# Where the stores of the sums of w_out are issued in the last pair of token tiles

## The chip, the cores and the metric

The kernel runs as one program on one core of a Trainium2 chip. The metric is the device time of one execution in microseconds (us), as a median over runs. Five engines each work through an instruction queue of their own in order: PE multiplies matrices, DVE (vector) and ACT (scalar) do elementwise work, POOL (GpSimd) a little of it, and SP only issues DMA transfers. An instruction waits in its queue until what it depends on has signalled, and everything behind it on that engine waits with it.

## The reference

An attention without a square matrix, and then a feed-forward layer:

```
q = softmax(q) over the 64 features of a head;  k = softmax(k) over the 576 positions
kv[b,h] = k^T v            (64 x 64 for each of 8 batches x 8 heads)
x = q kv, heads side by side:  4608 tokens x 512
h = x w_in                 (512 x 2048)
g = softplus(h)
out = g w_out              (2048 x 512)
```

All is float32. PE takes operands split in two parts, a high one (rounded to fp32r) and a low one (the remainder); three matmuls of parts (high by high, high by low, low by high) stand for one product.

## The kernel before

The 4608 tokens are nine tiles of 512 (numbers 0 to 8). Tiles 0 to 2 go one by one; tiles 3 to 8 go in pairs (3,4), (5,6), (7,8). In a pair the products with w_in are made in a scheme of seven products in place of eight for two by two blocks, on sums of blocks; the sums of w_in are made once and kept in DRAM. **In the last pair alone, (7,8), the products with w_out are made so too.** This needs, for each pair p of chunks of the hidden size (p = 0 to 7), four sums of blocks of w_out, "the sums of w_out", made by `turn_steps` (lines 1185 to 1211):

- `T0.p`, `whole_parts` (L1194): high plus low part of the loaded w_out, into a work tile called `two`, of which there is one
- `T1.p`, `combine` (L1199): four subtractions in that tile
- `T2.p`, `split` (L1204 on ACT, L1205 on DVE): a new tile `turned[p]` of 1 MB, in slot `x0` for even p and `x1` for odd p; ACT writes its high part, then DVE its low part
- `T3.p`, `store` (L1209 on SP): `turned[p]` to DRAM, for p = 0 to 5 alone, as `turn`

For p = 5, 6, 7 POOL does T0 and T1, and DVE otherwise. Tile 7's products read `turned[p]` one pass later (L1286). Tile 8's products come at the end of the kernel; for p = 0 to 5 they read the sums again from DRAM, loaded by step `R{p}` (`load_sources`, L1294 and L1295), which first waits until the two slots that it fills are free.

The work is written out as a sequence. The last pair runs in eight passes p = 0 to 7 of four steps k = 0 to 3, and after them come the products that are left. In each step PE's products with w_in (L1137) are issued, then the names in the plan's string ahead of its bar, then the products with w_out of the pass before (L1286), then the names behind the bar. The plan of the last pair is the third list in `PAIRS`; its first 32 strings are the steps of the eight passes. Each engine gets its instructions in the order in which the sequence calls them. In step 1 of a pass SP also issues the load of w_in's sums called `low` (L1073), in step 3 the load called `top` (L1073) ahead of the string and the load `down` of w_out (L1080) behind the products. A load waits for its slot to be free.

A slot is given to a new tile once all accesses to the old tile are done, also those that come later in the sequence than the new tile's first write: so T2.2's write to `x0` waits for the landing of store T3.0, though T3.0 stands behind it in the plan. The other names in the strings: S, J and L take w_in's products out of PSUM (L1398 ACT, L1401 DVE, L1404 and L1408 ACT), `a` and `e` make the operands of tiles 7 and 8 (L1239 ACT, L1240 and L1252 DVE), `v` adds up results (L1306 DVE).

Of the kernel before, what the change touches and what calls it, by code (L numbers as in the profile page):

```python
# [186 lines left out]
        "S3.1 J3.1|T1.1 v2.0",  # L187
        "a3.0 T2.1 L4.1|a0.1 a1.1 J2.1",
        "|S1.2 J1.2 a2.1 v3.0",
        "L3.1 L1.2 S2.2 T3.1 T0.2|",  # L190
        "S3.2 T1.2 J3.2|",
        "a3.1 L4.2 J2.2 v2.1 T2.2 L2.0|a0.2 T3.0",
        "|v3.1 T0.3 S1.3 J1.3 L2.1 a1.2 T1.3 a2.2 L1.3",
        "|S2.3 T2.3",
        "S3.3|J3.3",
        "v2.2 a3.2 L4.3|J2.3 a0.3",
        "T0.4 a1.3 S1.4 T3.3 T1.4 L2.3 J1.4 v3.2 a2.3 T3.2 e0.0 L3.3|",
        "S2.4 L2.2|",
        "|S3.4 J3.4 a3.3 v2.3",
        "|L1.4 J2.4 a0.4 L4.4",  # L200
        "T2.4 S1.5|J1.5",
        "v3.3 a1.4|S2.5",
        "L3.4 L2.4 a2.4 T3.4 S3.5 T0.5 J3.5|L3.2 T1.5",
        "e1.0 a3.4 T2.5 L1.5 v2.4 J2.5|v3.4 L4.5 a0.5",
        "S1.6 J1.6|",
        "L2.5 a1.5 S2.6|a2.5",
# [2 lines left out]
        "L1.6 T0.7 a0.6 L2.6 R0 v3.5 a1.6 S1.7 J1.7 L3.6 e0.6|T1.7 a2.6",  # L209
        "T2.7|S2.7 a3.6",  # L210
        "L1.7|S3.7 J3.7 e1.6 v2.6",
        "L4.7 T3.5 e2.6|J2.7",
        "L3.7 a0.7 a1.7 a2.7 R2 v3.6 a3.7|",
        "|",
        "|",
        "|",
        "e3.6|",
        "|",
        "L2.7|e0.7 T3.7 T3.6",
        "|",  # L220
        "|",
        "|e1.7",
# [72 lines left out]
def tile_attn_ffn(  # L295
# [362 lines left out]
    def eight(name, shape, dtype=F32):  # L658
        return (xp if name[0] == "x" else wp).tile(shape, dtype, name=name)
# [175 lines left out]
    with tc.manual_schedule():  # L835
# [127 lines left out]
        def dram(name, k, shape):  # L963
            drams[name, k] = dp.tile([P, *shape], F32, name=f"{name}{k}")
            return drams[name, k]
# [220 lines left out]
        def turn_steps(p, w):  # L1186

            work = []

            def whole_parts():  # L1190
                work.append(qp.tile([P, 2, TOK], F32, name="two").rearrange("p c (k n) -> p (c k) n", k=2))
                d = downs[w].bitcast(F32)
                y = work[0].rearrange("p (c k) n -> p c (k n)", c=2)
                (nc.gpsimd if p in TURN_POOL else nc.vector).tensor_tensor(out=y, in0=d[:, :, 0], in1=d[:, :, 1], op=ALU.add)  # L1194

            def combine():
                y = [work[0][:, i] for i in range(4)]
                for out, in0, in1 in ((0, 1, 0), (1, 3, 1), (3, 3, 0), (2, 3, 2)):
                    (nc.gpsimd if p in TURN_POOL else nc.vector).tensor_tensor(out=y[out], in0=y[in0], in1=y[in1], op=ALU.subtract)  # L1199

            def split():
                turned[p] = eight(f"x{p % 2}", [P, 2, 4, 256], F32R)
                hi, lo = (turned[p][:, i] for i in range(2))
                nc.scalar.copy(hi, work[0])  # L1204
                nc.vector.tensor_tensor(out=lo, in0=work[0], in1=hi.bitcast(F32), op=ALU.subtract)  # L1205

            def store():
                if p in SOURCE_SLOTS:
                    nc.sync.dma_start(out=dram("turn", p, [2, 4, 256]), in_=turned[p].bitcast(F32))  # L1209

            return [whole_parts, combine, split, store]

        def operand_set(name):

# [153 lines left out]
        for s, A in enumerate(firsts):  # L1368
# [24 lines left out]
            for p in range(NJ // 2):  # L1393
# [19 lines left out]
                if final:  # L1413
                    steps.update({f"T{k}.{p}": fn for k, fn in enumerate(turn_steps(p, 2 * s * (NJ // 2) + p))})
# [106 lines left out]
```

## Time and profile before

| | us |
|---|---|
| median of 3 runs | 850.25 (849.27 to 850.69) |
| the profiled execution's own time | 852.85 |
| its span, first to last instruction | 851.1 |
| PE busy | 814.8 (96%) |
| DVE busy | 640.1 (75%) |
| ACT busy | 532.8 (63%) |
| POOL busy | 89.1 (10%) |

The span is what the profile's views divide up; the profiled execution's own time is 1.75 us longer than its span, and 2.6 us above the median of the runs. The last pair's eight passes lie between 655 and 802 us of the span; behind them come the products that are left, to the end.

### The profile page before, as it was taken

How to read it: one execution, taken by the hardware profiler on the slowest of the kernel's cores; microseconds unless marked ns; L12 is line 12 of the kernel's file. 1: busy time of each engine (PE TensorE's matmuls, PEld its weight loads, DVE VectorE, ACT ScalarE, POOL GpSimd, SP SyncE). 2: the span in 40 equal slices, each digit the busy share in tenths (PEclk: the TensorE clock that was granted, in tenths of full speed). 3: DMA queues.
4: the chain of work that ended last, by engine and by line, in shares of the span. 5: the costliest groups of instructions: out<-in, count | busy, mean ns of one | idle time of the engine just before them, and what ended most of it. 6: DMA issues, size and time to landing. Idle time of an engine off the chain costs nothing.

```text
span 851.1 us, 12276 instructions
## 1 busy us (share of the span) xinstructions
PE 814.8 (96%) x4460; PEld 681.9 (80%) x4460; DVE 640.1 (75%) x1041; ACT 532.8 (63%) x895; POOL 89.1 (10%) x184
## 2 busy tenths in 40 slices
PE   5999999999999999999999999999999994996898
PEld 4778888888887778888888888888888883885898
DVE  8999978888978897677676965566668663676786
ACT  7999767757757775675676657555466542453422
POOL 1110001101141511100010001000000000052000
PEclk9999999999999999999999999999999996999799
DMA  9991143556647587576677566555574674875282
GB/s 346 374 366 47 36 137 106 192 187 228 203 140 245 187 311 270 194 264 220 201 276 273 187 235 222 181 215 198 201 252 180 231 248 133 280 267 173 100 327 107
DMA packets 84012, 181.68 MB, mean 213 GB/s; under 512 B 5360, under 2 KB 55792, under 8 KB 74224
## 3 DMA queue, kind: packets, MB, share of 16 engines
q1 hardware_dynamic: 83952, 180.90, 61.1%
q8 instruction: 35, 0.57, 0.3%
q14 instruction: 25, 0.20, 0.1%
HBM read 142.08 MB, written 38.80 MB: 213 GB/s over the span
## 4 chain that ended last, share of the span: by engine, by line
PE 83%; DVE 7%; ACT 4%; DMA 4%; issue 2%; SPq 1%; DVEq 0%; ACTq 0%
PE ph L1137 25%; PE po L1157 21%; PE po L1286 5%; PE ph L775 4%; PE ph L777 4%; PE ph L776 4%; PE po L810 4%; PE po L812 4%; PE po L811 4%; PE att L1286 3%; DMA turn<-x 2%; PE att L465 2%; PE att L691 1%; PE ph L1286 1%; PE po L808 1%
## 5 line engine op out<-in xcount | busy, mean ns | idle before, releaser
L1137 PE MATMUL ph<-w,w 128*128 128x512 f32 x864 | 215.0, 396 | 20.1 <-ACT w L1398 19.6
L1137 PEld LDWEIGHTS ph<-w,w 128*128 128x128 f32 x864 | 163.3, 191 | 56.0 <-ACT w L1398 20.4
L1157 PE MATMUL po<-w,g_hi 128*128 128x512 f32 x528 | 165.8, 390 | 0.0
L1157 PEld LDWEIGHTS po<-w,g_hi 128*128 128x128 f32 x528 | 98.7, 188 | 20.3
L1157 PE MATMUL po<-w,g_lo 128*128 128x512 f32 x264 | 103.0, 390 | 0.0
L1401 DVE TENSOR_TENSOR w<-ph,w 128x512 f32<-128x512 f32 x54 | 37.1, 688 | 52.1 <-PE ph L1137 29.2
L1398 ACT COPY w<-ph 128x512 f32<-128x512 f32 x54 | 31.5, 584 | 65.3 <-PE ph L1137 65.2
L810 PE MATMUL po<-w,g_hi 128*128 128x512 f32 x164 | 64.6, 394 | 0.0
L812 PE MATMUL po<-w,g_lo 128*128 128x512 f32 x164 | 64.0, 390 | 0.0
L811 PE MATMUL po<-w,g_hi 128*128 128x512 f32 x164 | 63.9, 390 | 0.0
L1157 PEld LDWEIGHTS po<-w,g_lo 128*128 128x128 f32 x264 | 49.6, 188 | 10.3
L775 PE MATMUL ph<-x,w 128*128 128x512 f32 x142 | 56.5, 398 | 0.0
L777 PE MATMUL ph<-x,w 128*128 128x512 f32 x142 | 55.4, 390 | 0.0
L776 PE MATMUL ph<-x,w 128*128 128x512 f32 x142 | 55.3, 390 | 0.0
L437 POOL PARTITION_ALL_REDUCE mb<-mx x28 | 26.2, 938 | 278.4 <-DVE mx L435 271.3
L790 DVE TENSOR_TENSOR g_lo<-w,g_hi 128x512 fp32r<-128x512 f32 x51 | 34.9, 687 | 20.8 <-ACT g_hi L789 17.3
L789 ACT CAST g_hi<-w 128x512 fp32r<-128x512 f32 x51 | 31.6, 619 | 29.8 <-PE po L1157 28.1
L685 DVE TENSOR_TENSOR two<-att,two 64x512 fp32r<-64x512 f32 x56 | 38.6, 689 | 13.3 <-ACT two L683 12.6
L683 ACT CAST two<-att 64x512 fp32r<-64x512 f32 x56 | 32.5, 580 | 13.2 <-DVE att L678 12.4
L783 ACT ACTIVATE l<-ph 128x512 f32<-128x512 f32 (+1 forms) x50 | 29.2, 584 | 18.2 <-PE ph L777 17.0
L435 DVE TENSOR_REDUCE mx<-kvt 128x128 f32<-128x640 f32 x28 | 37.0, 1325 | 4.7 <-DMA kvt<-in_kv_tail 4.5
L1404 ACT ACTIVATE w<-w 128x512 f32<-128x512 f32 x54 | 33.8, 630 | 7.6 <-DVE w L1401 7.4
(324 smaller groups left out, 1688.4 us busy)
## 6 DMA issues: line engine op xcount, KB each, us to landing
w<-down SPq DMA_DIRECT2D x40, 1024.0 KB, 6.2
w<-top SPq DMA_DIRECT2D x24, 1024.0 KB, 4.9
w<-low SPq DMA_DIRECT2D x24, 768.0 KB, 4.3
kvt<-in_kv SPq DMA_DIRECT2D x30, 512.0 KB, 5.6
w<-in_w_in SPq DMA_DIRECT2D x16, 512.0 KB, 9.6
w<-in_w_out SPq DMA_DIRECT2D x16, 512.0 KB, 10.1
q<-in_q SPq DMA_DIRECT2D x16, 512.0 KB, 5.2
down<-w SPq DMA_DIRECT2D x15, 512.0 KB, 5.0
```

The lines of the kernel that those rows point to most:

```text
L435: nc.vector.tensor_reduce(out=mx, in_=kt.rearrange("p c z d -> p z d c"), op=ALU.max, axis=AX.X)
L685: nc.vector.tensor_tensor(out=w[SIDE[1 - z], z], in0=ps[zs], in1=w[zs, z].bitcast(F32), op=ALU.subtract)
L775: nc.tensor.matmul(ph, lhsT=w_hi, rhs=x_hi, start=h == 0, stop=False)
L776: nc.tensor.matmul(ph, lhsT=w_lo, rhs=x_hi, start=False, stop=False)
L777: nc.tensor.matmul(ph, lhsT=w_hi, rhs=x_lo, start=False, stop=h == HP - 1)
L810: nc.tensor.matmul(po, lhsT=g_hi[:, ms], rhs=w_hi, start=j == chunks(t)[0], stop=False)
L811: nc.tensor.matmul(po, lhsT=g_hi[:, ms], rhs=w_lo, start=False, stop=False)
L812: nc.tensor.matmul(po, lhsT=g_lo[:, ms], rhs=w_hi, start=False, stop=j == chunks(t)[-1])
L1137: nc.tensor.matmul(bank, lhsT=a, rhs=b, start=start and e == k == 0, stop=e == 1 and k == 2, skip_group_check=True)
L1157: nc.tensor.matmul(po, lhsT=g[:, cs], rhs=w, start=first and k == 0, stop=end and k == 2)
L1286: nc.tensor.matmul(to, lhsT=g[:, m * P:(m + 1) * P], rhs=w, start=start and k == 0 and (m == 0 or len(banks_of) == 2), stop=k == 2, skip_g ...
L1401: nc.vector.tensor_tensor(out=l[k, p], in0=ph_b, in1=l[k, p], op=ALU.add)
```

## The change

The function `store` goes away and its one DMA is issued in `split`, directly behind the subtraction that makes the low part; the names T3.p go out of the plan. All instructions stay, and the order on PE, ACT, DVE and POOL; in SP's queue the six stores stand at other places.

```diff
-        "L3.1 L1.2 S2.2 T3.1 T0.2|",
+        "L3.1 L1.2 S2.2 T0.2|",
         "S3.2 T1.2 J3.2|",
-        "a3.1 L4.2 J2.2 v2.1 T2.2 L2.0|a0.2 T3.0",
+        "a3.1 L4.2 J2.2 v2.1 T2.2 L2.0|a0.2",
...
-        "T0.4 a1.3 S1.4 T3.3 T1.4 L2.3 J1.4 v3.2 a2.3 T3.2 e0.0 L3.3|",
+        "T0.4 a1.3 S1.4 T1.4 L2.3 J1.4 v3.2 a2.3 e0.0 L3.3|",
...
-        "L3.4 L2.4 a2.4 T3.4 S3.5 T0.5 J3.5|L3.2 T1.5",
+        "L3.4 L2.4 a2.4 S3.5 T0.5 J3.5|L3.2 T1.5",
...
-        "L4.7 T3.5 e2.6|J2.7",
+        "L4.7 e2.6|J2.7",
...
-        "L2.7|e0.7 T3.7 T3.6",
+        "L2.7|e0.7",
...
                 nc.vector.tensor_tensor(out=lo, in0=work[0], in1=hi.bitcast(F32), op=ALU.subtract)
-
-            def store():
                 if p in SOURCE_SLOTS:
                     nc.sync.dma_start(out=dram("turn", p, [2, 4, 256]), in_=turned[p].bitcast(F32))
 
-            return [whole_parts, combine, split, store]
+            return [whole_parts, combine, split]
```

## Rows read from the trace of the kernel before

**Rows 1.** The page: busy time, share of the span and instructions by engine.
```profile
PE   814.8 (96%) x4460; PEld 681.9 (80%) x4460; DVE 640.1 (75%) x1041; ACT 532.8 (63%) x895; POOL 89.1 (10%) x184
```

**Rows 2.** Windows, passes 2 to 7: length, busy times, granted clock, DMA share, GB/s.
```profile
687.68:702.28 14.60, 14.60 (x86) 12.91 (x85) 8.22 (x15) 4.98 (x9) 0.00 (x0) 1.00 0.76 255
702.28:730.50 28.22, 16.99 (x87) 14.18 (x86) 14.61 (x25) 8.69 (x15) 0.00 (x0) 0.76 0.44 147
730.50:745.10 14.60, 14.60 (x87) 12.92 (x86) 7.76 (x16) 6.66 (x13) 0.00 (x0) 1.00 0.94 327
745.10:759.70 14.60, 14.60 (x87) 12.92 (x86) 11.30 (x15) 8.27 (x15) 8.30 (x7) 1.00 0.83 268
759.70:775.77 16.07, 14.85 (x87) 12.97 (x85) 13.62 (x21) 8.23 (x15) 7.80 (x7) 1.00 0.42 149
775.77:801.75 25.98, 17.65 (x86) 15.17 (x85) 13.77 (x25) 8.66 (x16) 1.54 (x2) 0.80 0.54 183
```

**Rows 3.** The chain in order of time: start, us, what.
```profile
702.85 11.09 DMA turn<-x
...
778.14 9.93 DMA turn<-x
```

**Rows 4.** Timeline of PE: start, us, instructions, idle before and its releaser.
```profile
695.94 2.91 PE L1137 MATMUL ph<-w,w 128*128 128x512 f32 x12
...
716.42 6.46 PE L1137 MATMUL ph<-w,w 128*128 128x512 f32 x18 [11.23 <-ACT w L1398]
...
777.16 4.24 PE L1137 MATMUL ph<-w,w 128*128 128x512 f32 x18
789.73 2.93 PE L1137 MATMUL ph<-w,w 128*128 128x512 f32 x6 [8.33 <-ACT w L1398]
```

**Rows 5.** Waits from 640 to 851 us: total, times, longest.
```profile
ACT x L1204 <- DMA turn<-x: 28.6, 3, 15.9
```

**Rows 6.** Timeline of ACT.
```profile
697.53 0.60 ACT L1408 ACTIVATE w<-ph 128x512 f32<-128x512 f32 x1 [1.20 <-PE ph L1137]
714.02 1.04 ACT L1204 CAST x<-two 128x1024 fp32r<-128x1024 f32 x1 [15.89 <-DMA turn<-x]
...
744.66 1.05 ACT L1204 CAST x<-two 128x1024 fp32r<-128x1024 f32 x1 [3.72 <-DMA turn<-x]
...
778.77 0.41 ACT L1239 CAST w<-w 128x256 fp32r<-128x256 f32 x1 [0.30 <-PE ph L1137]
788.14 1.04 ACT L1204 CAST x<-two 128x1024 fp32r<-128x1024 f32 x1 [8.97 <-DMA turn<-x]
```

**Rows 7.** Timeline of DVE.
```profile
671.38 1.22 DVE L1205 TENSOR_TENSOR x<-two,x 128x1024 fp32r<-128x1024 f32 x1 [1.18 <-ACT x L1204]
...
715.10 1.23 DVE L1205 TENSOR_TENSOR x<-two,x 128x1024 fp32r<-128x1024 f32 x1 [14.92 <-ACT x L1204]
...
724.07 0.68 DVE L1401 TENSOR_TENSOR x<-ph,x 128x512 f32<-128x512 f32 x1
...
755.92 1.21 DVE L1205 TENSOR_TENSOR x<-two,x 128x1024 fp32r<-128x1024 f32 x1
...
780.64 0.88 DVE L1252 TENSOR_TENSOR w<-w,w 128x256 f32<-128x256 f32 x2
```

**Rows 8.** Timeline of POOL.
```profile
773.82 3.57 POOL L1199 TENSOR_TENSOR two<-two 128x256 f32<-128x256 f32 x4
```

**Rows 9.** Timeline of SP: DMAs issued.
```profile
672.17 0.33 SPq L1073 DMA_DIRECT2D w<-top  x1
...
702.48 0.32 SPq L1080 DMA_DIRECT2D w<-down  x1
...
776.01 1.60 SPq L1294 DMA_DIRECT2D w<-down  x2
```

**Rows 10.** DMA issues from 655 to 800 us: count, KB each, median us to landing.
```profile
w<-top SPq DMA_DIRECT2D x6, 1024.0 KB, 5.6
turn<-x SPq DMA_DIRECT2D x6, 1024.0 KB, 10.5
```

## The prediction

> **What bounds the kernel now.** I read the page first: PE is busy 96% of the span [rows 1], so time can come only from where PE stands still or runs slowly. Windows cut at the starts of PE's passes show where that is: passes 2, 4 and 5 take 14.60 us each, PE busy all through, the granted clock 1.00; pass 3 takes 28.22 us, pass 6 16.07 and pass 7 25.98, and in passes 3 and 7 the clock is 0.76 and 0.80 [rows 2]. A pass that only PE sets is thus 14.60 us, and 13.62 + 1.47 + 11.38 = 26.5 us lie above it in three passes.
>
> The chain in order of time names what ends last in passes 3 and 7: a store of sums, 11.09 and 9.93 us long, both times [rows 3]. The timeline of PE has the holes, 11.23 us ahead of 716.42 and 8.33 ahead of 789.73, each ended by ACT, which takes w_in's products out of PSUM [rows 4]. The waits say what held ACT: it waited three times, 28.6 us in all, for a landing of `turn` ahead of L1204, the high part of a new sum [rows 5]. On ACT's timeline these are the writes of sum 2 (at 714.02, after 15.89 us), sum 4 (744.66, 3.72) and sum 7 (788.14, 8.97) [rows 6]; each goes to the slot whose old sum is still being stored: stores 0, 2 and 5.
>
> Why those landings are late is seen on SP. Sum 0 was complete when DVE ended its low part at 671.38 + 1.22 = 672.60 [rows 7], but its store goes out at 702.85 [rows 3], right behind the load of 702.48 [rows 9], which PE's products had to release. Sum 5 was complete at 755.92 + 1.21 = 757.13 [rows 7]; its store goes out at 778.14 [rows 3], behind R0's loads, of which the first starts at 776.01 [rows 9]. So ACT waits for a store that waits in SP's queue for PE, and PE then waits for ACT.
>
> **The change part by part.** Six stores of 1 MB stay, and are issued earlier; no instruction comes or goes on other engines.
>
> *Store 0, and the stall of pass 3.* It moves from 702.85 to 672.60. With the median landing of 10.5 us [rows 10] it has landed at 683, with the longest transfer of a store that the chain shows (11.09) at 684. The write of sum 2 then waits for nothing: ACT is free at 697.53 + 0.60 = 698.1 [rows 6], so that it starts 15.9 us earlier. What is late next in this pass? DVE. Its work from sum 2's low part to the join that PE's last step of the pass needs ran from 715.10 to 724.75 without a pause, 9.65 us [rows 7]. Started behind ACT at about 700.2, with some 1.8 us of waits for PE's own results (an estimate from the starts in rows 2 and 4), it ends at 711.7. PE wants it for the second half of the 12 matmuls that start 8.26 us into a pass (695.94 - 687.68) [rows 2, 4], so 8.26 + 1.36 = 9.6 us into it, at 702.28 + 9.6 = 711.9. It just fits; I take no loss, and as the other end the 1.47 us that pass 6 lost with 13.62 us of DVE's work in it [rows 2]. So pass 3 falls to 14.60 us: **13.62 us**. That is 11.23 us of hole and about 2.2 us of slow clock: 18 matmuls took 6.46 us behind the hole, and 18 of the same form take 4.24 us in pass 7 ahead of its hole [rows 4].
>
> *Store 5, and the stall of pass 7.* It moves from 778.14 to 757.13 and is no longer behind R0. It lands at about 768 [rows 10]. ACT has its turn for sum 7 at 778.77 + 0.41 = 779.18 [rows 6]; POOL, which makes this sum, is done at 773.82 + 3.57 = 777.39 [rows 8]. So sum 7's write runs from 779.2 to 780.2, the copy of PSUM behind it (0.6 us) to 780.8, and PE, which ends its 18 matmuls at about 777.16 + 4.1 = 781.2 [rows 4], doesn't wait. Pass 7 falls from 25.98 to 14.60: **11.38 us**, of it 8.33 of hole and some 2.9 of slow clock (0.80 in this pass [rows 2]). DVE is next here too: 13.77 us of work in this pass [rows 2], with sum 7's low part right behind what ends at 781.52 [rows 7]. I take 0.3 us of loss, and keep 0 and the 1.47 us of pass 6 as ends.
>
> *Store 2, and the wait of 3.72 us in pass 4* [rows 6]. ACT and DVE get ahead by that much, but PE has no hole in passes 4 and 5 (14.60 us each [rows 2]): nothing on the path. It is cover for what follows. If DVE keeps the lead until pass 6, up to 1.47 us more could go; I count nothing, since ACT and DVE wait for PE again in between.
>
> *Stores 1, 3, 4.* No later instruction waits for them now; moved earlier they only land earlier.
>
> *The queue that they are moved past.* SP issues in order, so a store whose sum isn't ready holds the loads behind it. Sum 0 is ready at 672.60; the load of `top` behind it went out at 672.17 [rows 7, 9] and goes out 0.9 us later, the store's issue included. It lands 5.6 us on [rows 10] and is first used at 687.68, the start of pass 2 [rows 2]: 15.5 us from issue, so 9 us to spare. Nothing. Sum 2 is ready at about 701.4, ahead of the load of 702.48; sum 5 at 757.13, ahead of the load that follows pass 5's products at 759.70 [rows 2, 7, 9]. For sums 1, 3 and 4 the same holds by 2 us or more, worked out from the same distances in a pass. The Trainium skill states this ordering too, and it speaks against the change: "DMA: Bandwidth & Descriptors", section "Anatomy of one DMA", says that a transfer's wait for a semaphore is spent on the issuing sequencer ahead of dispatch, so an early store can block. The trace agrees (store 5 went out 21 us after its sum was complete). By that rule alone the price here would be the 0.9 us above, inside the 9 us to spare, so the sum is the same; it is the ground of the rival on the slower side.
>
> *The sum.* 13.62 + 11.38 - 0.3 = 24.7 us. The profiled execution took 852.85 us, and would take 828.15. It stands 2.6 us above the median of 850.25; the same gain from the median gives **825.6 us**. Ends: both DVE losses at 1.47 give 828.2; no loss and pass 6's excess gone too give 823.8. If the 2.6 us belong to the stalls (landings that were shorter in the other runs), the time is 828.2.
>
> **Rivals.**
>
> *One stall is replaced.* Sum 7's write needs POOL as well, and POOL ends only 1.8 us ahead of ACT's turn [rows 6, 8], while the profile calls POOL's spans rough; in pass 3 DVE fits by 0.2 us. If a new wait as long as the old takes one place, 850.25 - 13.62 = 836.6, or 850.25 - 11.38 = 838.9 us. Against: POOL or a landing would have to be 8 us later than any row shows.
>
> *The stores crowd the loads.* Each pass now has 768 KB and three transfers of 1024 KB, 3.9 million bytes, 269 GB/s over 14.60 us. If a load had a store's 10.5 us ahead of it on top of its own 5.6 [rows 10], 16.1 us against 14.60 from issue to use would cost 1.5 us in each of six passes: 834.6 us at most, some 831 for half. Against: pass 4 moved 327 GB/s at a DMA share of 0.94, and PE had no hole in it [rows 2].
>
> *It doesn't do what it says:* the writes of sums 2 and 7 also wait for the products that read the old sum, and if those end last, 850.3 us. Against: these are products of the pass before, and ACT resumed right at the stores' landings.
>
> *Slower.* SP's queue is the mechanism: a store that waits for DVE holds `low`, `top` and `down` behind it, and PE starves. The spare time of a load is 14.60 - 5.6 = 9 us; to eat the 24.7 us, each of six stores would have to hold its followers for 9 + 4.1 = 13.1 us. With 15 us it would be 825.6 + 6 x 6 = 861.6 us. The rows give 0.9 us at the worst.
>
> **How the numbers follow.** Forecast 0.74 (its own range 823.5 to 828.5), one stall replaced 0.12, crowded loads 0.08, no effect 0.03, slower 0.03. The range of 822.8 to 832 takes the forecast and about half of the crowding. A difference of 0.2% (1.7 us) is what a measurement of this kernel can tell from none. Faster by more: 0.74 + 0.12 + 0.08 = 0.94; same 0.03; slower 0.03.
>
> **What would show it.** Right: passes 3 and 7 at 14.6 to 16 us in windows at the starts of PE's passes, clock 1.00 in both; no wait of ACT's L1204 for `turn`; stores issued within 1 us of the end of DVE's L1205; DMA gone from the chain in the last pair. Pass 6 at about 16 us as before. Wrong: a hole of over 2 us on PE in passes 2 to 7, whatever ends it: POOL or DVE for the first rival, a load's landing for the second, and for the slower side loads on SP that are issued later in their pass than before.

## The result, and the profile after

The changed kernel takes 828.25 us (median of 4 runs, 827.57 to 829.52) against 850.4 us (median of 4, 849.27 to 850.69): the ratio is 0.9744, 95% interval 0.9727 to 0.9761. In a later job beside other kernels it took 827.7 us (5 runs) against 850.52 (9 runs), ratio 0.9732 (0.9713 to 0.9751). The profiled execution took 828.36 us with a span of 826.6; before it was 852.85 and 851.1. So the traces are 24.5 us apart, the medians 22.15 in one job and 22.8 in the other.

The page of the changed kernel, busy time by engine, to be read against [rows 1]: PE's busy time has fallen by 5.5 us, though its 4460 instructions are the same.

```profile
PE 809.3 (98%) x4460; PEld 678.3 (82%) x4460; DVE 638.6 (77%) x1041; ACT 533.0 (64%) x895; POOL 90.9 (11%) x184
```

Windows from the start of pass 2 to the end of pass 7, as in [rows 2]: passes 3 and 7, which took 28.22 and 25.98 us at clocks of 0.76 and 0.80, take 14.62 and 14.60 at 1.00. Pass 6 is as it was.

```profile
687.86:702.46 14.60, 14.60 (x87) 12.92 (x86) 9.70 (x17) 6.74 (x12) 0.00 (x0) 1.00 0.75 276
702.46:717.08 14.62, 14.62 (x86) 12.84 (x85) 13.19 (x23) 6.88 (x12) 0.00 (x0) 1.00 0.89 343
717.08:731.68 14.60, 14.60 (x86) 12.93 (x85) 8.92 (x17) 7.15 (x13) 1.08 (x1) 1.00 0.57 200
731.68:746.28 14.60, 14.60 (x86) 12.93 (x85) 8.82 (x14) 7.67 (x14) 6.80 (x7) 1.00 0.83 257
746.28:762.36 16.08, 14.86 (x86) 12.98 (x85) 14.09 (x21) 8.22 (x15) 7.45 (x7) 1.00 0.57 207
762.36:776.96 14.60, 14.60 (x86) 12.93 (x85) 13.15 (x25) 8.72 (x16) 1.55 (x2) 1.00 0.75 253
```

SP's timeline has five of the six stores right where their low parts end, and the loads around them (before: [rows 3, 9]). Store 0 goes out at 672.81 and store 5 at 743.61; the load of `top` behind store 0 is 0.8 us later in its pass than before, the one of w_out that follows 1.2 us; in passes 2 to 7 no load is later. Store 4 misses the prediction's sign of 1 us: DVE's low part of sum 4 ended at 730.45, and the store went out 1.84 us later, right behind the load of 731.88, which stands ahead of it in SP's queue. No DMA is left in the chain of the last pair.

```profile
672.81 0.33 SPq L1207 DMA_DIRECT2D turn<-x  x1
673.18 0.43 SPq L1073 DMA_DIRECT2D w<-top  x1
...
685.68 0.32 SPq L1207 DMA_DIRECT2D turn<-x  x1
...
701.51 0.32 SPq L1207 DMA_DIRECT2D turn<-x  x1
702.65 0.32 SPq L1080 DMA_DIRECT2D w<-down  x1
...
711.36 0.32 SPq L1207 DMA_DIRECT2D turn<-x  x1
...
731.88 0.32 SPq L1080 DMA_DIRECT2D w<-down  x1
732.29 0.38 SPq L1207 DMA_DIRECT2D turn<-x  x1
...
743.61 0.32 SPq L1207 DMA_DIRECT2D turn<-x  x1
```

```profile
729.23 1.22 DVE L1205 TENSOR_TENSOR x<-two,x 128x1024 fp32r<-128x1024 f32 x1
```

ACT's timeline, the writes of sums 2, 4 and 7 that waited for stores in [rows 6]: no bracket behind them now, that is, no idle time ahead of them that the view lists.

```profile
698.20 1.04 ACT L1204 CAST x<-two 128x1024 fp32r<-128x1024 f32 x1
...
727.42 1.04 ACT L1204 CAST x<-two 128x1024 fp32r<-128x1024 f32 x1
...
765.68 1.05 ACT L1204 CAST x<-two 128x1024 fp32r<-128x1024 f32 x1
```

PE's timeline has two holes left between 688 and 782 us, both ended by DVE: the one of pass 6 that was there before, and one of 0.60 us among the products behind pass 7, where it was 0.31 (the last line is from the kernel before).

```profile
761.54 0.50 PE L1284 MATMUL att<-w,g_hi 128*128 128x256 f32 x2 [1.22 <-DVE w L1304]
...
778.44 0.95 PE L1284 MATMUL att<-w,l 128*128 128x256 f32 x6 [0.60 <-DVE x L1304]
```

```profile
802.94 0.95 PE L1286 MATMUL att<-w,l 128*128 128x256 f32 x6 [0.31 <-DVE x L1306]
```

### The profile page after: what moved, and what is told of

It reads as the page before. It is cut to its first block, busy times and chain, and to the rows that moved or that the text cites. A ratio compares the mean times of both kernels' runs of the same rounds, so it can differ in the third digit from the quotient of the medians.

```text
span 826.6 us, 12278 instructions
## 1 busy us (share of the span) xinstructions
PE 809.3 (98%) x4460; PEld 678.3 (82%) x4460; DVE 638.6 (77%) x1041; ACT 533.0 (64%) x895; POOL 90.9 (11%) x184
## 4 chain that ended last, share of the span: by engine, by line
PE 86%; DVE 7%; ACT 2%; DMA 2%; issue 2%; SPq 1%; DVEq 0%; ACTq 0%
PE ph L1137 27%; PE po L1157 22%; PE po L1284 5%; PE ph L775 4%; PE ph L776 4%; PE ph L777 4%; PE po L810 4%; PE po L811 4%; PE po L812 4%; PE att L1284 3%; PE att L465 2%; PE att L691 1%; PE ph L1284 1%; DMA w<-in_w_out 1%; PE po L808 1%
## 5 line engine op out<-in xcount | busy, mean ns | idle before, releaser
L1137 PE MATMUL ph<-w,w 128*128 128x512 f32 x864 | 210.9, 391 | 0.5 <-DVE w L1026 0.5
L1137 PEld LDWEIGHTS ph<-w,w 128*128 128x128 f32 x864 | 161.1, 188 | 34.9 <-DVE w L1026 1.0
L437 POOL PARTITION_ALL_REDUCE mb<-mx x28 | 29.1, 1044 | 278.2 <-DVE mx L435 260.2
## 6 DMA issues: line engine op xcount, KB each, us to landing
w<-in_w_out SPq DMA_DIRECT2D x16, 512.0 KB, 10.1
```

What stands on the lines that cost most here:

```text
L1137: nc.tensor.matmul(bank, lhsT=a, rhs=b, start=start and e == k == 0, stop=e == 1 and k == 2, skip_group_check=True)
```

## The experiments

**One store at a time.** The first four kernels are the kernel before with only some stores moved:

```diff
+EARLY = (0,)          # or (5,), (0, 5), (1, 3, 4)
...
                 nc.vector.tensor_tensor(out=lo, in0=work[0], in1=hi.bitcast(F32), op=ALU.subtract)
+                if p in EARLY:
+                    nc.sync.dma_start(out=dram("turn", p, [2, 4, 256]), in_=turned[p].bitcast(F32))
...
             def store():
-                if p in SOURCE_SLOTS:
+                if p in SOURCE_SLOTS and p not in EARLY:
```

They ran in one job, with 13 runs of the kernel before (median 851.09, 849.0 to 852.53).

*Store 0 alone.*

> Only store 0 moves behind its low part; the other five stay where they were. Theory (two separate stalls, each from one store that waits in SP's queue): pass 3 falls from 28.2 to 14.6 us, pass 7 stays at about 26 us, and the time is 12 to 13.6 us below the kernel before, 837 to 838.5. Rival (the gain needs all stores moved, since they share SP's queue and the transfer engines): less than 8 us, above 842. Rival (the 2 us by which the medians' gain of 22.2 fell short of the traces' gain of 24.5 sit in this stall): 11 us or less, above 839.

838.91 us, ratio 0.9861 (0.9841 to 0.988), 12.2 us faster. The gain is inside what was expected, and the time 0.4 us above it. Windows of its passes 3 and 7, PE's hole in pass 7, and in the chain the store that ends it: the first stall is gone, the second is left.

```profile
702.51:717.13 14.62, 14.62 (x87) 12.85 (x86) 13.19 (x23) 6.88 (x12) 0.00 (x0) 1.00 0.57 206
762.40:787.23 24.83, 16.70 (x86) 14.33 (x85) 13.78 (x25) 8.66 (x16) 1.54 (x2) 0.86 0.57 191
```

```profile
776.16 2.93 PE L1138 MATMUL ph<-w,w 128*128 128x512 f32 x6 [8.13 <-ACT w L1401]
```

```profile
764.44 10.06 DMA turn<-x
```

*Store 5 alone.*

> Only store 5 moves. Theory: pass 7 falls from 26.0 to about 14.6 us, pass 3 stays at about 28 us; the time is 9.5 to 11.4 us below before, 839 to 841. Rival (all must move): less than 6 us, above 844. If the two gains of the single moves add up to that of the whole change (22.2 us), the stalls are independent.

839.47 us, ratio 0.9867 (0.9846 to 0.9888), 11.6 us faster, 0.2 us more than was expected at most. Windows of passes 3 and 7, and in the chain the store that still ends pass 3's hole:

```profile
702.52:728.94 26.42, 16.48 (x86) 13.76 (x85) 14.61 (x25) 8.69 (x15) 0.00 (x0) 0.81 0.46 151
774.22:788.82 14.60, 14.60 (x86) 12.92 (x85) 13.39 (x25) 8.72 (x16) 1.54 (x2) 1.00 0.76 253
```

```profile
703.09 9.80 DMA turn<-x
```

*Stores 0 and 5.*

> Stores 0 and 5 move, the other four stay. Theory (stores 1 to 4 are off the path): the time of the changed kernel, 828.3, within 0.7 us; the write of sum 4 may wait some 3 us for store 2 with PE going on. Rival (the lead of ACT and DVE from store 2 is part of the gain): 1.5 us or more above the changed kernel.

828.0 us, ratio 0.9736 (0.9717 to 0.9755): the time of the whole change. The two single gains add up to 23.8 us, both together gave 23.1; with a scatter of 3.5 us among the runs of the kernel before, that is the same. ACT's write of sum 4 waited for store 2 as expected, and PE went on; its hole among the products behind pass 7 is 0.31 us, as before:

```profile
731.39 1.05 ACT L1205 CAST x<-two 128x1024 fp32r<-128x1024 f32 x1 [3.78 <-DMA turn<-x]
```

```profile
778.23 0.95 PE L1289 MATMUL att<-w,l 128*128 128x256 f32 x6 [0.31 <-DVE x L1309]
```

*Stores 1, 3 and 4.*

> Stores 1, 3 and 4 move, 0, 2 and 5 stay. Theory: no later instruction waits for these three, so the time of the kernel before, 850.4, within 0.8 us. Rival (early stores alone take transfers out of the crowded stretch behind 702 us, so that store 0 lands sooner): 1 to 4 us below before, with a hole in pass 3 shorter than 11.2 us by that much.

851.25 us (10 runs, 848.78 to 853.72), ratio 1.0 (0.9987 to 1.0014). These moves are worth nothing, within some 1.2 us either way. The windows of passes 3 and 7, the stores in the chain, and PE's hole behind pass 7:

```profile
702.85:729.23 26.38, 17.63 (x87) 14.61 (x85) 14.80 (x25) 8.69 (x15) 0.00 (x0) 0.81 0.54 189
774.50:799.22 24.72, 16.56 (x87) 14.17 (x86) 13.42 (x25) 8.66 (x16) 1.54 (x2) 0.86 0.58 191
```

```profile
703.41 8.61 DMA turn<-x
...
776.69 9.95 DMA turn<-x
```

```profile
800.70 0.95 PE L1289 MATMUL att<-w,l 128*128 128x256 f32 x6 [0.60 <-DVE x L1309]
```

Store 0 landed 2.5 us sooner than in [rows 3], and the hole of pass 3 was as much shorter, as the rival had it for this one trace, but the median time did not follow. In the kernel with store 5 alone moved, where stores 1, 3 and 4 stand at their old places, it landed 1.3 us sooner too. The landing of a store behind the load of 702 us thus differs, from 8.6 to 11.1 us over these three traces. They are of three kernels, so how much of it is scatter of one kernel and how much the other stores is not shown.

**The plan's place or the queue.** The kernel before with one word changed:

```diff
             def store():
                 if p in SOURCE_SLOTS:
-                    nc.sync.dma_start(out=dram("turn", p, [2, 4, 256]), in_=turned[p].bitcast(F32))
+                    nc.gpsimd.dma_start(out=dram("turn", p, [2, 4, 256]), in_=turned[p].bitcast(F32))
```

> All six stores stand at the plan places of the kernel before, but are issued from POOL's queue in place of SP's. POOL has nothing else between 640 and 747 us, so store 0 goes out behind store 1, at about 686 us, and no longer behind the load of 702; store 5 stands on POOL behind its work on sum 7, which ends at about 777. Theory (what delayed store 0 was the place in SP's queue, not the plan's place by itself): pass 3 falls to 14.6 to 16 us, pass 7 keeps its hole of 8 to 11 us, and the time is that of the kernel with store 0 alone moved, 837 to 841. Rival (a store issued at that plan place is late on any queue, or the plan's place binds the new sum's write in another way): pass 3 keeps its hole, 849 us or more.

842.47 us (841.54 to 845.28) against 851.72 in its job, ratio 0.9906 (0.9877 to 0.9936). Pass 3 lost its hole with the store at the same place in the plan: store 0 went out on POOL at 685.14 with store 1. Pass 7 kept its hole, since store 5 stood on POOL behind sum 7's work. A window of pass 3, then PE's holes, then POOL's timeline:

```profile
701.63:716.26 14.63, 14.63 (x87) 12.87 (x86) 13.20 (x23) 6.89 (x12) 1.06 (x2) 1.00 0.72 270
```

```profile
747.21 0.51 PE L1286 MATMUL att<-w,g_hi 128*128 128x256 f32 x2 [2.18 <-DVE w L1306]
...
778.77 2.93 PE L1137 MATMUL ph<-w,w 128*128 128x512 f32 x6 [8.56 <-ACT w L1398]
```

```profile
685.14 1.42 POOL L1209 DMA_DIRECT2D turn<-x  x2 [162.62 <-DVE x L1205]
...
729.92 0.53 POOL L1209 DMA_DIRECT2D turn<-x  x1 [18.07 <-DVE x L1205]
737.58 2.39 POOL L1194 TENSOR_TENSOR two<-w 128x1024 f32<-128x1024 f32 x1 [7.13 <-issue]
```

So it was the place in SP's queue that delayed store 0. The time is 1.5 us above what I had expected at most, because of a cost that I had not seen: behind store 4, POOL began sum 5 only 7.13 us later, waiting for nothing that the trace shows, and DVE and PE came late in passes 5 and 6 (the hole of 2.18 us, and one of 1.69).

**Twice the stores.** The changed kernel with the store written a second time to another buffer:

```diff
                     nc.sync.dma_start(out=dram("turn", p, [2, 4, 256]), in_=turned[p].bitcast(F32))
+                    nc.sync.dma_start(out=dram("again", p, [2, 4, 256]), in_=turned[p].bitcast(F32))
```

> The changed kernel with every store of sums issued twice in a row, the second to a buffer that nothing reads: 6 MB more to DRAM in 90 us. Theory (stores behind their low part have over 20 us to land before the slot is wanted, and loads have 9 us to spare): the time of the changed kernel, 828.3, within 0.7 us. Rival (stores crowd the loads; the changed kernel is at the edge): 1.5 us or more per pass that has a store, 834 to 840, with PE waiting on a landing of low, top or down.

828.01 us (median of 4), ratio 0.9738 (0.9705 to 0.977); three runs within 827.5 to 828.1 and one of 832.6. Windows of passes 2, 3, 6 and 7: 408 GB/s at a DMA share of 1.00 in pass 2, and PE still without a hole in passes 2 and 3.

```profile
688.10:702.70 14.60, 14.60 (x87) 12.91 (x86) 9.69 (x17) 6.74 (x12) 0.00 (x0) 1.00 1.00 408
702.70:717.32 14.62, 14.62 (x86) 12.86 (x85) 13.19 (x23) 6.89 (x12) 0.00 (x0) 1.00 1.00 401
...
746.52:761.12 14.60, 14.60 (x86) 12.92 (x85) 12.60 (x21) 8.97 (x16) 4.42 (x5) 1.00 0.82 325
761.12:776.65 15.53, 14.89 (x86) 12.84 (x85) 14.26 (x25) 7.92 (x15) 4.34 (x5) 1.00 0.70 237
```

In this trace POOL began its work on sum 7 1.8 us later in pass 6 than in the changed kernel (13.06 us into it, against 11.27). Pass 6 lost its excess, and pass 7 took 15.53 us, with a hole of 0.64 us in which ACT waited for POOL's sum 7: the first rival of the prediction in small. What held POOL is the load of w_out that sum 7 is made from, as far as the rows go. Issued at 746.71, it took 12.7 us to land, that is until 759.4, and POOL began at 759.58; in the changed kernel it was issued at 746.48 and took 7.9 us (first line, then the doubled stores). The trace names an instruction of DVE (L1305) as what ended POOL's wait, but in the changed kernel POOL began ahead of that instruction. So the stores did crowd a load here, which is the second rival, and not at a cost that the median shows. What made the one run of 832.6 I did not try.

```profile
w<-down SPq DMA_DIRECT2D x1, 1024.0 KB, 7.9
```

```profile
w<-down SPq DMA_DIRECT2D x1, 1024.0 KB, 12.7
```

**What is left of pass 6.** The changed kernel with two neighbours in the plan exchanged:

```diff
-        "L3.5 a3.5 T0.6 T1.6 S3.6 J3.6 e2.0 T2.6|e3.0 v2.5",
+        "L3.5 a3.5 T0.6 T1.6 S3.6 J3.6 e2.0 T2.6|v2.5 e3.0",
```

> The changed kernel, in pass 6 the result step v2.5 ahead of e3.0 on DVE (both neighbours in the plan). It looks at the 1.47 us that pass 6 still takes above 14.60: PE waits 1.22 us for v2.5, which stands behind two subtractions that take 3.50 us while POOL runs. Theory (the order on DVE makes the wait): pass 6 falls to 14.6 to 14.9 us; DVE has less lead in pass 7, where the wait of 0.6 us ahead of the last products grows to at most 1.4; the time falls by 0.4 to 1.2 us, 827 to 827.9. Rival (DVE's amount of work binds passes 6 and 7 together): the wait only moves, and the time stays at 828.3 within 0.3.

827.12 us (826.26 to 827.59), ratio 0.9714 (0.9693 to 0.9735), in a job without the changed kernel. So both were run side by side.

> The changed kernel again, beside the swap, so that the two can be compared on one chip: 828.0 within 0.8 us.

> The swap of v2.5 and e3.0 again, beside the changed kernel. Theory (DVE's order makes the 1.22 us of wait in pass 6, and about 0.2 us come back in pass 7): 0.6 to 1.2 us below the changed kernel, about 827.1. Rival (the first 0.9 us was scatter between jobs): within 0.3 us of it.

The changed kernel took 827.7 us (827.52 to 828.14), the swap 827.12 again (826.76 to 827.51). The two sets of runs are apart by 0.01 us only, and the medians by 0.58 us, just under what was expected at least: a small gain, on few runs. The traces show where it is from. DVE in the first trace of the swap, PE's only hole left in passes 2 to 7 and the products behind, and the windows of passes 6 and 7:

```profile
757.64 0.68 DVE L1304 SCALAR_TENSOR_TENSOR w<-att,w 128x512 f32<-128x512 f32 x1
758.24 3.66 DVE L1238 TENSOR_TENSOR q<-w,q 128x512 fp32r<-128x512 f32 x2
```

```profile
777.68 0.95 PE L1284 MATMUL att<-w,l 128*128 128x256 f32 x6 [0.60 <-DVE x L1304]
```

```profile
746.55:761.15 14.60, 14.60 (x87) 12.92 (x86) 12.62 (x19) 7.98 (x14) 6.14 (x6) 1.00 0.63 231
761.15:776.20 15.05, 15.05 (x86) 12.76 (x85) 14.31 (x27) 8.68 (x16) 2.88 (x4) 1.00 0.68 244
```

The result step now stands ahead of the two subtractions, the hole of 1.22 us is gone, and the last one did not grow. Pass 6 lost 1.48 us, but pass 7 took 0.45 us more, so the rival holds for a third of it: some of the wait only moved. This kernel has the lowest median of all that were run.

## Why the prediction was right

**The stall of pass 3.** The step held: store 0 went out at the end of its sum, ACT wrote sum 2 at 698.20 (forecast 698.1) and the pass took 14.62 us. The close fit with DVE was real. DVE's join ended at 711.94, 9.48 us into the pass (711.7 forecast, which is 9.4 into it), and PE's 12 matmuls of that step took 0.04 us longer than in [rows 4]; the pass lost 0.02 us of the 1.47 kept as an end. The join on DVE, and then the 12 matmuls on PE:

```profile
711.25 0.69 DVE L1399 TENSOR_TENSOR x<-ph,x 128x512 f32<-128x512 f32 x1
```

```profile
710.72 2.95 PE L1137 MATMUL ph<-w,w 128*128 128x512 f32 x12
```

**The stall of pass 7.** It went whole: the pass took 14.60 us. ACT began sum 7 with no wait, 1.7 us behind the end of POOL's work (forecast 1.8):

```profile
760.42 3.57 POOL L1199 TENSOR_TENSOR two<-two 128x256 f32<-128x256 f32 x4
```

The 0.3 us that DVE's load would cost here did not come. The products behind the pass lost as much, where the hole of 0.31 us became 0.60, but for another reason: with stores 0 and 5 alone moved pass 7's stall was gone too, and the hole stayed at 0.31; with stores 1, 3 and 4 moved the stall stood, and the hole was 0.60. That this term met the trace is luck.

**The other four stores.** Off the path, as counted: moved alone, three of them gave a ratio of 1.0, and with stores 0 and 5 moved the rest added nothing that the medians show (828.0 and 828.25 us). Store 2's wait of 3.7 us stayed hidden.

**SP's queue, and crowding.** Both rivals were priced by the spare time of the loads, and with the six stores that spare time is there: in passes 2 to 7 no hole of PE ends with a load's landing. The most that a load went out later in its pass is 1.2 us, the one of w_out behind store 0, above the 0.9 of the prediction. Even with every store doubled, nothing of PE's time in passes 2 to 5 was lost; in pass 7 the spare time had then run out, by a load that took 4.8 us longer. The slower side did not show. Half of the crowding would have been 830.1 us and not the 831 of the prediction; its range does not change by it.

**The size.** Within the traces the sum was 24.7 us and came out at 24.5. Carried over to the medians it was too large: 22.15 and 22.8 us, so that 825.6 became 828.25. The terms that were mis-sized are those of both stalls, 13.62 and 11.38 us, taken from one execution that was a long one. In the two other traces with store 0 at its old place pass 3 took 26.42 and 26.38 us, which makes 11.8 us of gain. In two other traces with store 5 at its old place on SP pass 7 took 24.83 and 24.72 us, which makes 10.2 and 10.1. From the kernel with stores 1, 3 and 4 moved, which has both stalls in one trace, the sum would have been 21.9 us. In pass 3 the landing of store 0 was shorter, 9.80 and 8.61 us against 11.09. In pass 7 it was not: 10.06 and 9.95 us against 9.93. There the holes differ by 0.2 us at most, and the rest is PE's slow stretch behind the hole: PE was busy for 16.70 and 16.56 us at a clock of 0.86, against 17.65 at 0.80 [rows 2]. Why that stretch was longer in one execution is not shown. In the medians the stores moved singly gave 12.2 and 11.6 us.

The prediction had this as an end (828.2) and not as its value; the profiled time beside the median had said that this execution was a long one. The runs fit this, though their numbers differ: the kernel before scatters over 3.5 us (13 runs), the changed kernel over 0.6 us (5 runs of the second job) to 2 us (4 runs of the first).

**The clock.** Behind each hole PE ran slowly for a stretch, and that went with the hole: passes 3 and 7 have a granted clock of 1.00 where they had 0.76 and 0.80, and PE's busy time fell by 5.5 us, against 2.2 + 2.9 = 5.1 forecast. Right behind the hole of 11.23 us, in which PE stood still, the clock granted was 0.50, that is 1.2 GHz of its two levels:

```profile
716.42:719.00 2.58, 2.58 (x6) 1.83 (x6) 2.58 (x5) 1.00 (x2) 0.00 (x0) 0.50 0.01 3
```

The rows show that the slow stretch and the hole do not add up simply. In pass 3, with store 5 alone moved, the hole was 9.94 us and PE was busy for 16.48; with stores 1, 3 and 4 moved it was 8.75 and 17.63. The pass took 26.42 and 26.38 us.

## What to carry to other kernels

A store of a finished tile belongs where the tile is finished when the tile's slot will be written again: put later in the sequence, it inherits every wait of the loads ahead of it in the same issuing queue, and the engine that wants the slot waits in turn. To find such a store, read what ends the longest waits, and then compare the time at which the stored data were complete with the time of issue; a gap of 20 or 30 us is the queue, not the transfer. Where a stall contains a transfer's landing and a slow stretch of PE behind it, size it from more than one execution before the gain is counted: here the landing differed by up to 2.5 us from trace to trace, and the slow stretch by up to 1.1.

## What the runs showed of the hardware

- After a store issued from POOL, POOL stood still for longer than the store's own row says: 0.53 us of issue, and then 7.13 us until the next instruction, with no releaser. For 3.4 us of that DVE was idle, waiting for PE. The Trainium skill, "SBUF — State Buffer", section "SBUF: two separate sides", says that transfers issued from this queue have their descriptors made on GpSimd, and that some DVE instructions lock it out meanwhile; DVE's idle time in the trace says that the lock alone does not explain it. It was seen once, and its cause is not shown.
- Two subtractions of DVE (128x512, both inputs in SBUF) took 3.50 us while POOL worked and 1.28 us in the trace with the doubled stores, where POOL began later, behind a load that landed later. So a change in DMA traffic alone moved PE's hole from one pass to the next.
- The landing of a 1 MB store at the same place of the sequence ranged from 8.61 to 11.09 us in three executions, of three kernels that differ in their other stores.
- Holes of 8.33, 8.13 and 8.16 us in pass 7 were followed by slow stretches of different length: PE's busy time in the pass was 17.65, 16.70 and 16.56 us.
